# Attention interleaved with a SwiGLU block on one core: split gate and up operands made anew in the second half, stack loads by eight, attention steps spread over both halves, transposes one step later

## The chip, the cores and the metric

The kernel runs on one core of a Trainium2 chip. The metric is device time in microseconds (us) of one launch. Before the change three runs gave 1970.26, 1974.51 and 1974.52 us; the median is 1974.51 us. The core has a matrix engine (PE, with its weight loads listed as PEld), a vector engine (DVE), a scalar engine (ACT), a general engine (POOL) and a sync engine (SP), which in this kernel issues every DMA. Each engine works through its own instructions in order and waits where a semaphore says so.

## The reference, cut to what matters

```
x = A_x                                     # 2048 tokens, D = 576
g = sigmoid((x * gate_w).sum(-1))           # one gate per token
a = attention(x, wq, wk, wv, beta) @ wo     # 32 heads of 18, four segments of 512 tokens,
                                            # causal softmax inside a segment, plus a memory
                                            # read from the segments before it
b = (silu(x @ w_gate) * (x @ w_up)) @ w_down   # hidden width 4608
out = g * a + (1 - g) * b
```

All of it is float32. The kernel reaches that accuracy by splitting an operand into a rounded high part and a low part (the rest) and adding three products: high by high, high by low and low by high.

## The kernel before, in words

**Stages.** First comes a stage of about 230 us that makes queries, keys, values and the memory. It writes each query and key channel as three bfloat16 terms to a DRAM tensor `stk` (line 74; the stores are queued at lines 356 to 359) and the values to `vd`. Then come 72 tiles of the SwiGLU block with the attention woven in, and last a stage that multiplies by `wo` and mixes (lines 1085 to 1118).

**The SwiGLU tiles.** The loop at line 983 runs over two halves of 36 tiles. A half takes 1024 tokens as two blocks of 512, a tile takes 128 hidden channels, and both halves need the same weights. Gate and up weights of a tile, cut into two halves of 256 input channels, form a two by two block matrix. It is multiplied with the tokens by seven products instead of eight (`seven`, line 970): each product has six matmuls of 512 columns (line 975) and a seventh for the last 64 input channels (line 978). The seven left operands are sums and differences of weight blocks, each split into high and low. `w_make` (line 235) makes them: two raw weight loads of 256 KB each (`w_load`, line 198), four sums on POOL (line 243), seven high parts on ACT (line 247), seven low parts on DVE (line 250). It serves the first half only, where `keep` (line 253) also stores the seven operands of 256 KB each to DRAM (`wc`). In the second half `w_fetch` (line 690) loads them back, seven loads a tile (line 695). The operand pool `wop` has seven buffers, the raw pool four.

**The down product.** Every third tile (`q == 0`, called a group tile here) the hidden results of the three tiles before it are multiplied with `w_down` in 16 groups of nine matmuls (`down_group`, line 824). Three tiles, one of them a group tile, are called a triple here.

**The attention.** `att_gen` (line 782) is a generator. Two heads are a unit of five banks, and there are 64 units, so 320 banks. One step takes several banks each one stage further: `s_bank` multiplies queries and keys (PE, line 710) and takes the row maximum (DVE, line 716); `e_bank` takes the exponential (ACT, line 728) into a tile `pe` and masks it (POOL, line 736); `p_bank` makes a float16 high part (DVE, line 742) and low part (POOL, line 743) in a tile `p`, three steps after its scores (`PL`); `x_bank` transposes `p` by a DMA into `pt` (line 747), four steps after its scores (`XL`); `v_unit` multiplies with the values (PE, lines 758 and 759) and sums three terms (DVE, line 765), seven steps after the last scores of its unit (`VL`). The pool has 4 `pe`, 3 `p` and 8 `pt` buffers. For each unit the queries and keys are loaded from `stk` as a stack of 108 rows by ten DMAs (`stack_loads`, line 174; issued at line 790).

**What sets the order.** The order is written out by hand. A tile calls `tick` eight times, once after each product and once more, and `tick` calls `beat` (line 920). A beat first runs what was deferred to it (the parts of `w_make`, the loads, the splits), then its share of down groups (`SHARE`), and after every second of these an attention step if credit is there. Credit per slot comes from `TICK[half]`: the second number where down groups are pending, the first in other tiles. In the first half only beats 2 to 7 earn credit, and in a tile without groups beats 5 and 6 earn none (`QUIET`). With the numbers before, that gives 10 steps in a group tile and none in the others in the first half, 12 and four or five in the second half, and the attention ends in tile 31 of the second half. When the generator is empty, `c_open` (line 847) frees its pools and defers the loads for the last stage. SP gets its DMAs in that same order and starts none before the one ahead of it.

**The function tables of ACT.** Silu and exp need different tables. `exp_table` (line 967) runs a one element exp, so that the switch back from silu comes at a chosen place. Before the change it stands after the silu pair in every tile of the second half and in the group tiles of the first, and at the end of every third tile of the first half (line 1065).

## Time and profile before

| | |
|---|---|
| median of three runs | 1974.51 us (1970.26 to 1974.52) |
| profiled execution | 1969.58 us, of it span 1967.6 us |
| mean granted clock of PE | 0.973 |
| instructions | 35841 |
| matmuls | 11868 |
| DMA | 435.10 MB in 579305 packets |

The profile of one execution lists the instructions of each engine with start, duration and idle time ahead, and what ended that idle time. Times inside it count from the start of the span. The span is the time from the first to the last instruction; 1.98 us of the execution lie outside. Line 1032 (an ACT copy) runs once in each of the 72 tiles, at the end of the first product, so its starts mark the tiles. Line 742 (a DVE cast) runs once for each attention bank, so its count is the number of steps in a window. SP's instructions have no busy share; their rows show how long SP took to issue a DMA, not how long the transfer took.

### The profile page before, as it was taken

How to read it: one execution, taken by the hardware profiler on the slowest of the kernel's cores; microseconds unless marked ns; L12 is line 12 of the kernel's file. 1: busy time of each engine (PE TensorE's matmuls, PEld its weight loads, DVE VectorE, ACT ScalarE, POOL GpSimd, SP SyncE). 2: the span in 40 equal slices, each digit the busy share in tenths (PEclk: the TensorE clock that was granted, in tenths of full speed). 3: DMA queues.
4: the chain of work that ended last, by engine and by line, in shares of the span. 5: the costliest groups of instructions: out<-in, count | busy, mean ns of one | idle time of the engine just before them, and what ended most of it. 6: DMA issues, size and time to landing. Idle time of an engine off the chain costs nothing.

```text
span 1967.6 us, 35841 instructions
## 1 busy us (share of the span) xinstructions
PE 1777.4 (90%) x11868; PEld 1516.8 (77%) x11868; DVE 1222.8 (62%) x3001; ACT 999.6 (51%) x1927; POOL 824.3 (42%) x1058
## 2 busy tenths in 40 slices
PE   9999999898999999999888788788888878989999
PEld 7888887787878887788767676676766756768899
DVE  6655677675777676777755565555655655664445
ACT  7765565555555565555553544435544444454421
POOL 4443533453445444454444444444444444441021
PEclk9999999999999999999999999999998989989999
DMA  7644689889988898888998888979888798888634
GB/s 272 228 147 167 214 263 285 236 200 268 282 242 213 247 279 262 229 228 255 296 256 184 229 192 203 200 193 235 208 196 224 169 233 192 202 228 215 205 131 139
DMA packets 579305, 435.10 MB, mean 221 GB/s; under 512 B 418865, under 2 KB 461105, under 8 KB 579121
## 3 DMA queue, kind: packets, MB, share of 16 engines
q1 hardware_dynamic: 579120, 432.82, 80.8%
q8 instruction: 94, 1.54, 0.3%
q14 instruction: 91, 0.74, 0.1%
HBM read 210.32 MB, written 138.48 MB: 177 GB/s over the span
## 4 chain that ended last, share of the span: by engine, by line
PE 51%; DMA 22%; DVE 8%; issue 6%; ACT 5%; SPq 4%; POOL 4%; DVEq 0%; ACTq 0%; POOLq 0%
PE bank L975 21%; DMA pt<-p 15%; PE bank L834 13%; PE bank L137 8%; PE bank L978 3%; POOL p L743 2%; DMA draw<-in_wd_dram 2%; DVE p L742 2%; PE bank L710 2%; SPq L790 1%; SPq L747 1%; DVE ya L839 1%; PE bank L758 1%; DVE scr L716 1%; ACT L968 1%
## 5 line engine op out<-in xcount | busy, mean ns | idle before, releaser
L743 POOL TENSOR_TENSOR p<-pe,p 128x512 f16<-128x512 f32 x320 | 382.0, 1194 | 477.2 <-DVE p L742 476.9
L834 PE MATMUL bank<-dw,hh 128*128 128x320 f32 (+1 forms) x2304 | 496.0, 308 | 33.1 <-DVE ya L839 27.3
L834 PEld LDWEIGHTS bank<-dw,hh 128*128 128x128 f32 x2304 | 382.1, 191 | 58.2 <-DVE ya L839 40.1
L728 ACT ACTIVATE pe<-bank,mb 128x512 f32<-128x512 f32 (+3 forms) x512 | 244.9, 523 | 284.1 <-DVE mb L716 240.4
L834 PE MATMUL bank<-dw,hl 128*128 128x320 f32 (+1 forms) x1152 | 342.0, 297 | 0.3 <-DVE hl L115 0.3
L742 DVE CAST p<-pe 128x512 f16<-128x512 f32 x320 | 141.5, 442 | 303.8 <-DMA pt<-p 302.0
L716 DVE CUSTOM_DVE_ANT_0 scr<-bank,cm 128x512 bf16<-128x512 f32 (+3 forms) x512 | 246.2, 481 | 10.3 <-PE bank L710 3.4
L834 PEld LDWEIGHTS bank<-dw,hl 128*128 128x128 f32 x1152 | 219.5, 191 | 0.9 <-DVE hl L115 0.9
L978 PE MATMUL bank<-xr,rh 128*128 128x512 f32 x504 | 202.2, 401 | 9.2 <-DMA rh<-rc 9.1
L839 DVE TENSOR_TENSOR ya<-bank,ya 128x320 f32<-128x320 f32 x352 | 155.1, 451 | 82.9 <-PE bank L834 82.2
L736 POOL TENSOR_SCALAR_AFFINE_SELECT pe<-pe 128x256 f32<-128x256 f32 (+1 forms) x320 | 145.2, 454 | 105.0 <-ACT pe L728 103.0
L758 PE MATMUL bank<-v,pt 128*128 128x57 bf16 x1280 | 83.5, 190 | 55.5 <-DMA pt<-p 55.5
L1042 ACT ACTIVATE row<-bank 128x512 f32<-128x512 f32 x72 | 43.1, 599 | 172.4 <-PE bank L978 172.3
L710 PE MATMUL bank<-kst,qst 108*128 108x512 bf16 (+3 forms) x512 | 127.3, 310 | 3.7 <-DMA kst<-stk 2.8
L758 PEld LDWEIGHTS <-pt 128*128 128x128 f16 x1280 | 72.3, 97 | 70.1 <-DMA pt<-p 59.0
L243 POOL TENSOR_TENSOR ws<-raw 128x256 f32<-128x256 f32 x72 | 64.5, 896 | 145.1 <-DMA raw<-in_wf_dram 103.5
L978 PEld LDWEIGHTS bank<-xr,rh 128*128 128x128 f32 x504 | 97.9, 194 | 33.0 <-DMA rh<-rc 11.7
L918 DVE TENSOR_TENSOR hl<-row,hh 128x512 fp32r<-128x512 f32 x120 | 106.6, 888 | 20.9 <-ACT hh L917 20.5
L1032 ACT ACTIVATE bank<-bank 128x512 f32<-128x512 f32 x72 | 41.9, 581 | 131.3 <-PE bank L978 122.5
L1046 ACT ACTIVATE bank<-bank 128x512 f32<-128x512 f32 x72 | 41.9, 583 | 121.9 <-PE bank L978 121.6
L1047 DVE TENSOR_TENSOR row<-bank,row 128x512 f32<-128x512 f32 x72 | 49.6, 689 | 59.2 <-ACT bank L1046 59.2
L137 PE MATMUL bank<-xo,qhi 128*128 128x512 f32 x264 | 83.1, 396 | 0.0
(1689 smaller groups left out, 3869.7 us busy)
## 6 DMA issues: line engine op xcount, KB each, us to landing
rh<-rc SPq DMA_DIRECT2D x72, 336.0 KB
dc<-dw SPq DMA_DIRECT2D x36, 576.0 KB
dw<-dc SPq DMA_DIRECT2D x36, 576.0 KB
raw<-in_wf_dram SPq DMA_DIRECT2D x72, 256.0 KB
stk<-q SPq DMA_DIRECT2D x32, 384.0 KB
draw<-in_wd_dram SPq DMA_DIRECT2D x36, 288.0 KB
rc<-rt SPq DMA_DIRECT2D x42, 224.0 KB
vd<-vps SPq DMA_DIRECT2D x8, 912.0 KB
```

The lines of the kernel that those rows point to most:

```text
L137: nc.tensor.matmul(t, st[n], mv[n], start=(n == 0), stop=(n == 13))
L710: nc.tensor.matmul(t[:, c:c + w], qs[:KR, pr, P * i:P * i + P], ks[:KR, pr, 0:w], start=True, stop=True)
L716: nc.vector.tensor_tensor_reduce(scr[:, :w], t[:, c:c + w], cm[:, L - w:L], -SCALE, 3.0e38, OP.add, OP.min, m[:, k:k + 1])
L728: nc.scalar.activation(pe[:, c:c + w], t[:, c:c + w], AF.Exp, bias=m[:, k:k + 1], scale=SCALE)
L736: nc.gpsimd.affine_select(d, d, pattern=pat, compare_op=OP.is_ge, fill=0.0, base=0, channel_multiplier=1)
L742: nc.vector.tensor_copy(p[:, 0], pe)
L743: nc.gpsimd.tensor_sub(p[:, 1], pe, p[:, 0])
L758: nc.tensor.matmul(t[:, pr, i, :], pt[:, c], v, start=(n == 0), stop=False, skip_group_check=True)
L834: nc.tensor.matmul(t, p, q[:, cs], start=(n == 0), stop=(n == 3 * CH - 1))
L839: nc.vector.tensor_add(ya[:, i, cs], t, ya[:, i, cs])
L975: nc.tensor.matmul(t, w[:, p, z], x[z][:, q], start=first and n == 0, stop=False, skip_group_check=True)
L978: nc.tensor.matmul(t, rem[:, RPOS[j]], XR[j], start=False, stop=True, skip_group_check=True)
```

## The change

Six things change.

- In the second half only the first two tiles (`KEPT = 2`) load their operands from `wc`. For the other 34 tiles `w_make` runs again: raw loads, sums, high and low parts, without the stores. In the first half only the first two tiles store theirs.
- `TICK` changes, so that each tile of the first half that is no group tile gets two attention steps (a group tile 10 as before), and in the second half a group tile gets 10 and the others two or three.
- The stack of a unit is loaded by eight DMAs instead of ten, with the same rows. The first one of each kind takes 54 rows for both heads; for that the six pairs of terms are put in another order and the key terms are stored in reverse (`stk_store`).
- The transposes are issued five steps after the scores instead of four (`XL`), the product with the values follows eight steps after instead of seven (`VL`).
- There are 4 `p` buffers instead of 3, and 3 `pe` buffers instead of 4.
- `exp_table` stands after the silu pair in every tile of both halves.

With the new `TICK` and `VL` the attention has 333 steps instead of 332 and ends in tile 35 of the second half, the last one.

```diff
--- before.py
+++ after.py
@@ -37,10 +37,11 @@
 NB = 8 * NSEG
 NST = 2
 PL = 3
-XL = 4
-VL = 7
+XL = 5
+VL = 8
+KEPT = 2
 HALF = ((2, 3), (0, 1))
-TICK = ((0.0, 1.0), (0.76, 1.0))
+TICK = ((0.5, 1.0), (0.4, 0.85))
 QUIET = (5, 6)
 LEAD = 3
 SHARE = (0, 0, 2, 2, 3, 3, 3, 3)
@@ -73,7 +74,7 @@
     dram = pool(ctx, "dram", 1, space=bass.MemoryType.DRAM)
     stk = dram.tile([2, NSEG, D, 3, L], BF, name="stk")
     vd = dram.tile([NSEG, 2, P, 4, 16, 3, E], BF, name="vd")
-    wc = dram.tile([FT, 7, P, 4 * P], F32, name="wc")
+    wc = dram.tile([KEPT, 7, P, 4 * P], F32, name="wc")
     rc = dram.tile([FT // 4, 96, 4, 7 * P], F32, name="rc")
     xrd = dram.tile([7, P, L], F32, name="xrd")
     dc = dram.tile([FT, P, 2 * D], F32, name="dc")
@@ -173,20 +174,19 @@
 
     def stack_loads(u):
         s, b = divmod(u, 16)
-        q, k = (stk[kind, s, 2 * b * DH:2 * b * DH + 2 * DH].rearrange("(j r) z n -> r j z n", r=DH)
-                for kind in range(2))
-        tq, tk = qst[u % NST], kst[u % NST]
         r = []
-        for pr in range(2):
-            for z, n in ((0, 3), (1, 2)):
-                r0 = (0, 3 * DH)[z]
-                qz = q[:, pr, z]
-                r += [(tq[r0:r0 + n * DH, pr],
-                       bass.AP(tensor=qz.tensor, offset=qz.offset, ap=[qz.ap[0], [0, n]] + list(qz.ap)[1:])),
-                      (tk[r0:r0 + n * DH, pr], k[:, pr, 0:n])]
-            if pr == 0:
-                r += [(tq[5 * DH:KR], q[:, :, 2]), (tk[5 * DH:KR], k[:, :, 0])]
+        for kind, t, terms in ((0, qst, (0, 0, 1)), (1, kst, (2, 1, 2))):
+            d = stk[kind, s, 2 * b * DH:2 * b * DH + 2 * DH]
+            r.append((t[u % NST][0:3 * DH], d.rearrange("(j r) z n -> (r z) j n", r=DH)))
+            for n, z in enumerate(terms):
+                r.append((t[u % NST][(3 + n) * DH:(4 + n) * DH], d[:, z].rearrange("(j r) n -> r j n", r=DH)))
         return r
+
+    def stk_store(kind, s, a, b, q3):
+        d = stk[kind, s, a:b]
+        if kind:
+            d = bass.AP(tensor=d.tensor, offset=d.offset + 2 * L, ap=[d.ap[0], [-L, 3], [1, L]])
+        return d, q3
 
     def v_fetch(k):
         VP[k] = ap.tile([P, 4, 8, 3, E], BF, name="v")
@@ -232,9 +232,9 @@
     def r_fetch(f):
         nc.sync.dma_start(f32(rhs[f % 2][:96]).rearrange("p j n -> p (j n)"), rc[f // 4, :, f % 4])
 
-    def w_make(f):
+    def w_make(half, f):
         g, u = wraw_of.pop(f)
-        ops = wops[0, f] = [None] * 7
+        ops = wops[half, f] = [None] * 7
         a11, a12, a21, a22 = g[:, 0:2], g[:, 2:4], u[:, 0:2], u[:, 2:4]
         src = [a11, None, None, a12, None, None, a22]
 
@@ -257,8 +257,9 @@
                 (LEAD + 2, lambda: total(4, lambda: a11, lambda: a21)),
                 (LEAD + 4, lambda: total(5, lambda: a12, lambda: src[2]))]
         for j in range(7):
-            todo += [(LEAD + j, lambda j=j: high(j)), (LEAD + j + 2, lambda j=j: low(j)),
-                     (LEAD + j + 3, lambda j=j: keep(j))]
+            todo += [(LEAD + j, lambda j=j: high(j)), (LEAD + j + 2, lambda j=j: low(j))]
+            if half == 0 and f < KEPT:
+                todo.append((LEAD + j + 3, lambda j=j: keep(j)))
         return sorted(todo, key=lambda t: t[0])
 
 
@@ -353,10 +354,10 @@
             if ph is not None:
                 nc.vector.scalar_tensor_tensor(ph, t, 0.0, ph, op0=OP.max, op1=OP.add)
             if m < 4:
-                late.append((stk[u, s, m * P:m * P + P], q3))
+                late.append(stk_store(u, s, m * P, m * P + P, q3))
             else:
                 for kind in range(2):
-                    late.append((stk[kind, s, 512:D], q3[64 * kind:64 * kind + 64]))
+                    late.append(stk_store(kind, s, 512, D, q3[64 * kind:64 * kind + 64]))
 
         def v_step(s, hf, i):
             n = 288 + 2 * hf
@@ -636,7 +637,7 @@
                 wraw_of[0] = [w_load(0, u) for u in range(2)]
                 for z in range(2):
                     rhs.append(wop.tile([P, 7, P], F32R, name=f"rh{z}", bufs=1))
-                start = w_make(0)
+                start = w_make(0, 0)
             for n in range(8):
                 hf, i = divmod(n, 4)
                 flush()
@@ -721,7 +722,7 @@
             u, n = divmod(z, 5)
             m = mbs[u % 2]
             t = cur.pop(("t", z))
-            pe = ap.tile([P, L], F32, name="pe", bufs=4)
+            pe = ap.tile([P, L], F32, name="pe", bufs=3)
             for c, pr, i in SPLAN[n]:
                 w = P * (i + 1)
                 k = pr * 4 + i
@@ -738,7 +739,7 @@
 
         def p_bank(z):
             pe = cur.pop(("e", z))
-            p = cur["p", z] = ap.tile([P, 2, L], F16, name="p", bufs=3)
+            p = cur["p", z] = ap.tile([P, 2, L], F16, name="p", bufs=4)
             nc.vector.tensor_copy(p[:, 0], pe)
             nc.gpsimd.tensor_sub(p[:, 1], pe, p[:, 0])
 
@@ -786,7 +787,7 @@
                 if tau % 10 == 4 and sends:
                     nc.sync.dma_start(*sends.pop(0))
                 if n in (2, 3) and u + 1 < 2 * NB:
-                    for d in stack_loads(u + 1)[6 * (n - 2):4 * n - 2]:
+                    for d in stack_loads(u + 1)[4 * (n - 2):4 * n - 4]:
                         nc.sync.dma_start(*d)
                 z = tau - VL
                 if z % 20 == 0 and 0 <= z < N and z // 20 + 1 < 4 * NSEG:
@@ -989,15 +990,15 @@
                 groups += feed(half, f - 1)
             plan = []
             if nxt:
-                plan += w_make(nxt[1]) if nxt[0] == 0 else w_fetch(nxt[1])
+                plan += w_fetch(nxt[1]) if nxt[0] and nxt[1] < KEPT else w_make(*nxt)
                 if nxt != (0, 1):
                     plan.append((1 if nxt[1] else 10, lambda f=nxt[1]: r_fetch(f)))
                 for n, h in enumerate(BLOCKS.get(pos, ())):
                     plan += r_block(h, 4 * n)
-                if half == 0 and f + 2 < FT:
+                if f + 2 < FT:
                     wraw_of[f + 2] = [None, None]
                     for u in range(2):
-                        plan.append(((2, 5)[u], lambda u=u, f=f: wraw_of[f + 2].__setitem__(u, w_load(f + 2, u))))
+                        plan.append(((2, 5)[u] if f or not half else 5 + u, lambda u=u, f=f: wraw_of[f + 2].__setitem__(u, w_load(f + 2, u))))
             if pos == FT - 2:
                 X2, XR2 = [[None, None] for _ in range(7)], [None] * 7
                 plan += [(o + 8, fn) for o, fn in x_second(X2, XR2)]
@@ -1049,8 +1050,7 @@
             nc.scalar.activation(sg0, sg0, AF.Silu)
             seven(y, 5, False)
             nc.scalar.activation(sg1, y, AF.Silu)
-            if half or q == 0:
-                exp_table()
+            exp_table()
             tick()
             tick()
             seven(xx, 6, False)
@@ -1062,8 +1062,6 @@
                 split_by(2, hh[:, 0], hl[:, 0], sg0)
             split_by(3, hh[:, 1], hl[:, 1], sg1)
             tick()
-            if half == 0 and q == CH - 1:
-                exp_table()
             assert not groups
             if f == FT - 1:
                 groups += feed(half, f)
```

## The prediction

> **What bounds the kernel now.** I read the page first, then the starts of the 72 tiles, windows of whole triples, and SP's rows.
>
> ```profile
> span 1967.6 us, 35841 instructions
> PE 1777.4 (90%) x11868; PEld 1516.8 (77%) x11868; DVE 1222.8 (62%) x3001; ACT 999.6 (51%) x1927; POOL 824.3 (42%) x1058
> PE 51%; DMA 22%; DVE 8%; issue 6%; ACT 5%; SPq 4%; POOL 4%; DVEq 0%; ACTq 0%; POOLq 0%
> ```
>
> PE is busy for 90%, yet the chain that ended last lies on PE for only 51%, and on DMA for 22%. That is an average over unlike stages, so I cut the span at tile starts (line 1032).
>
> ```profile
> L1032 ACT ACTIVATE bank<-bank x31: 577/579/582, 266.8 to 898.6; 128x512 f32<-128x512 f32 x31
> ...
> L1032 ACT ACTIVATE bank<-bank x28: 582/582/598, 1035.1 to 1763.9; 128x512 f32<-128x512 f32 x28
> ...
> L742 DVE CAST p<-pe x96: 413/423/1314, 286.0 to 874.2; 128x512 f16<-128x512 f32 x96
> ...
> L742 DVE CAST p<-pe x191: 412/427/810, 1037.2 to 1762.8; 128x512 f16<-128x512 f32 x191
> ```
>
> 31 starts are 30 tiles, ten triples of the first half: 631.8 / 10 = 63.2 us each, with 9.6 attention steps. 28 starts are nine triples of the second half: 728.8 / 9 = 81.0 us each, with 21.2 steps. What would PE alone need? The end of the second half, where the attention is over, shows it, and one group tile with ten steps beside it (start and end, length, busy time and count of PE, PEld, DVE, ACT and POOL, granted clock, DMA share, GB/s):
>
> ```profile
> 1799.50:1810.60 11.10, 11.10 (x51) 9.19 (x49) 4.12 (x7) 7.29 (x12) 0.90 (x2) 1.00 0.95 298
> 1822.80:1853.50 30.70, 30.70 (x194) 28.34 (x193) 13.89 (x27) 9.35 (x15) 1.98 (x2) 1.00 0.48 139
> 898.60:933.30 34.70, 34.47 (x288) 31.18 (x287) 26.95 (x76) 16.70 (x36) 19.05 (x26) 1.00 0.80 202
> ```
>
> A bare tile is 11.1 us, a bare group tile 30.7, the group tile with ten steps 34.7: a step costs PE 0.40 us, and a triple with n steps has a floor of 52.9 + 0.40 n. The first half loses 63.2 - 56.7 = 6.5 us a triple, the second 81.0 - 61.4 = 19.6 us. The question is what takes the 19.6.
>
> ```profile
> DVE p L742 <- DMA pt<-p: 251.6, 111, 4.9
> ...
> SPq L747 <- POOL pe L736: 59.5, 71, 2.0
> SPq L747 <- POOL p L743: 19.0, 21, 1.8
> ```
>
> ```profile
> 1100.42 0.38 SPq L695 DMA_DIRECT2D wo__13533<-wc  x1
> 1100.85 0.80 SPq L790 DMA_DIRECT2D qst<-stk  x1
> 1101.71 0.48 SPq L790 DMA_DIRECT2D kst<-stk  x1
> 1102.24 0.78 SPq L790 DMA_DIRECT2D qst<-stk  x1
> 1103.06 0.75 SPq L790 DMA_DIRECT2D kst<-stk  x1
> 1103.85 0.48 SPq L790 DMA_DIRECT2D qst<-stk  x1
> 1104.38 0.31 SPq L790 DMA_DIRECT2D kst<-stk  x1
> 1104.79 1.27 SPq L747 DMA_TRANSPOSE pt<-p  x1
> ```
>
> ```profile
> L747 SPq DMA_TRANSPOSE pt<-p x192: 1231/1267/3547, 1033.6 to 1762.6; - x192
> ...
> L790 SPq DMA_DIRECT2D qst<-stk x190: 411/776/1823, 1044.6 to 1757.3; - x190
> L790 SPq DMA_DIRECT2D kst<-stk x190: 283/487/1345, 1045.4 to 1758.2; - x190
> ```
>
> In the nine triples (728.8 us) DVE stands for 251.6 us before the cast of line 742, because a transpose that must free a `p` buffer has not landed. The transposes are late because **SP is full**: its rows stand back to back, with 0.03 to 0.10 us between them. By medians it issues 192 x 1.267 = 243 us of transposes, 190 x 0.776 + 190 x 0.487 = 240 us of stack loads, and 189 operand loads (seven in each of 27 tiles) of 0.4 to 0.5 us, some 85 us. With some 80 other DMAs (half a microsecond each) and 0.08 us between all 840, that is about 675 of the 728.8 us, and at line 747 it waits for POOL in much of the rest (59.5 and 19.0 us). So the second half runs at the pace of SP, not of PE.
>
> **The change part by part.**
>
> *Operands made anew.* In 34 tiles of the second half seven loads become two, and 34 x 7 stores leave the first half. 476 transfers of 256 KB go and 68 come: 125 MB less and 18 MB more, of 435. What making them costs, the first half shows:
>
> ```profile
> 266.80:898.60 631.80, 85.02 (x210) 0.98 0.88 248
> ...
> 266.80:898.60 631.80, 104.85 (x212) 0.98 0.88 248
> ...
> 266.80:898.60 631.80, 105.15 (x120) 0.98 0.88 248
> ...
> 266.80:898.60 631.80, 74.62 (x156) 0.98 0.88 248
> ```
>
> These are the same window for line 247 (ACT, 0.405 us each), line 250 (DVE, 0.495), line 243 (POOL, 0.876) and line 728 (ACT exponentials, 74.62 / 96 = 0.78 us a step). A tile of the second half gains 7 x 0.405 = 2.8 us on ACT, 3.5 on DVE, 3.5 on POOL. In a group tile (ACT 16.7 us of 34.7 above) that lies beside PE. In the other tiles ACT is the engine to watch: the bare tile has 7.3 us, its tables included; plus 2.8, plus 2 to 2.5 steps at 0.78, that is 11.7 to 12.1; PE needs 11.1 + 2.5 x 0.40 = 12.1. A tile of the second half with three steps shows the same from the other end:
>
> ```profile
> 1022.60:1035.10 12.50, 12.50 (x63) 9.29 (x62) 8.52 (x23) 10.08 (x18) 4.95 (x7) 1.00 0.92 241
> ```
>
> PE fills its 12.5 us; with the operands made anew ACT has 10.1 + 2.8 = 12.9 and DVE 8.5 + 3.5 = 12.0; POOL has room (5.0 + 3.5). So PE, ACT and DVE stand abreast there.
>
> *Tables.* In the first half ACT now switches in all tiles: 12 more switches to silu and 12 back, inside the 7.3 us above.
>
> ```profile
> L1049 ACT ACT_TABLE_LOAD x60 | 77.0, 1283 | 1.1
> L968 ACT ACT_TABLE_LOAD x60 | 77.0, 1283 | 0.8
> ```
>
> That is 2.6 us in each of 12 tiles. The Trainium skill, "ScalarE: Activation LUTs", section "What ACT_TABLE_LOAD costs", gives 1283 ns for the load, as here, and 1380 ns for a drain on top. By that sentence each non-group tile would hold 2.8 us more ACT time. The rows show 0.8 and 1.1 us idle before all 60 loads of a kind together, so the sum here goes without the drain.
>
> *Even steps, SP's load.* A triple now has 14 or 15 steps. SP's part of a second half triple becomes 15 x 1.27 = 19.0 us of transposes, three stacks of eight loads, six raw loads and about eight others at half a microsecond, with 0.08 between some 53: about 42 us. The new loads (54 rows for both heads, 18 rows for both heads) have no row of their own; the stack rows bound them by 0.28 and 0.80 us, 6.7 to 19.2 us a triple. I take 0.5, nearest to the key row's 0.487; either way SP ends below 50 us. The first half has three `w_down` loads and stores and the blocks of line 226 more, and 21 stores less: under 50. SP no longer sets the pace.
>
> *Transposes a step later, buffers.* A transpose may wait a step longer for POOL, and the fourth `p` buffer gives DVE the same two steps until the buffer is needed: I count nothing beyond the 78.5 us of SP's waits, which lie in the 81.0. With three `pe` buffers instead of four the exponential waits for the subtraction of the step just before:
>
> ```profile
> ACT pe L728 <- POOL p L743: 33.1, 31, 2.8
> ...
> L743 POOL TENSOR_TENSOR p<-pe,p 128x512 f16<-128x512 f32 x320 | 382.0, 1194 | 477.2 <-DVE p L742 476.9
> ...
> L736 POOL TENSOR_SCALAR_AFFINE_SELECT pe<-pe 128x256 f32<-128x256 f32 (+1 forms) x320 | 145.2, 454 | 105.0 <-ACT pe L728 103.0
> ```
>
> The round is 0.78 (ACT) + 0.45 (mask) + 1.19 = 2.4 us, and in the dense part of a group tile steps come every 34.7 / 10 = 3.5 us or faster. It fits if DVE's cast is not late; bounds 0 and, if it is late as now, the third rival.
>
> *Stores of reversed keys.* The same bytes in three pieces a row, in a stage where SP and DMA have room; nothing, at most a few us.
>
> *The sum.* I take 36.5 us for a group tile (between 34.7 and 38.7) and 13.2 for the others (between 12.1 and 20.0): ACT's 12.9, and 0.3 for waits.
>
> ```profile
> 327.50:366.20 38.70, 36.26 (x287) 32.47 (x286) 26.01 (x76) 17.69 (x38) 20.63 (x32) 0.96 0.88 211
> 1241.80:1261.80 20.00, 15.39 (x98) 11.45 (x96) 10.27 (x28) 10.71 (x19) 8.22 (x12) 0.91 0.87 205
> ```
>
> The first is a group tile, the second a tile of the second half under SP's pace, which goes. I lean to the tile of 12.5 us above. A triple is then 36.5 + 2 x 13.2 = 63 us (floor 58.9). By stretches:
>
> ```profile
> L1032 ACT ACTIVATE bank<-bank x4: 582/582/582, 984.7 to 1035.1; 128x512 f32<-128x512 f32 x4
> ...
> L1032 ACT ACTIVATE bank<-bank x5: 582/582/582, 1799.5 to 1864.6; 128x512 f32<-128x512 f32 x5
> ```
>
> - up to 266.8: five steps and a few tables more, +4
> - first half, ten triples: 630 instead of 631.8, -2
> - 898.6 to 1035.1 (a triple, the break, three tiles without groups): 3 more in the first, 50 us to 40 in the last, -7
> - second half, nine triples: 567 instead of 728.8, -162
> - 1763.9 to 1864.6 (five tiles, before with seven steps in all): 113 instead of 101, +12
> - the end: two steps more; and the loads for `wo` start in the last tile instead of tile 31, so part of them is bare: +2 and +4
>
> That is -149: a span of 1819, 1821 us with the 2 us outside. The profiled execution (1969.6) lies 4.9 us under the median of the runs; I add most of that back and **forecast 1825 us**.
>
> **The rivals.** *ACT lags in the non-group tiles.* Two engines abreast with waits between them lose more than half a microsecond. At 15.5 us 47 tiles add 2.3 us each: 1825 + 108 = 1933. For it: ACT's order is fixed, and the two silus with two table loads of 1.28 us stand as one block in it. By the drain that the page of the Trainium skill states the tile would be 13.2 + 2.8 = 16.0, and the time 1957 (0.02 of this case's chance). Against: the 12.5 us row.
>
> *A step costs the same wherever it stands* (the slower side). From 63.2 us at 9.6 steps to 81.0 at 21.2 the slope is 1.53 us a step. If that belongs to the loop of cast, subtraction, transpose and buffer, not to SP, then moving steps moves their price: ten triples +67, the triple after +6, the three tiles -8, nine triples -85, the last two triples +35, start and end +12: +27, and the 4 to the median: 2001 us. It decides from 69.8 us a triple on (63 + 149 / 22). For it: DVE's 251.6 us at that very buffer. Against: SP's rows without a gap.
>
> *Three `pe` buffers bind.* POOL waits 476.9 us for the cast, 1.5 us a step. If that passes to ACT in the ten steps of 22 group tiles, and a third of it to PE, the group tiles take 5 us longer each: 1825 + 110 = 1935. Against: with SP free the cast waits less.
>
> *The operands come late all the same.*
>
> ```profile
> POOL ws L243 <- DMA raw<-in_wf_dram: 90.3, 13, 10.9
> ```
>
> In the first half POOL waits 90.3 us in 30 tiles for raw loads, 3.0 a tile. If 33 tiles of the second half pay that on PE: 1825 + 99 = 1924. Against: with 107 MB less to move the loads land sooner.
>
> **How the numbers follow.** Forecast (1780 to 1880) 0.66; ACT lags 0.11; `pe` binds 0.06; operands late 0.05; steps cost the same 0.12. Within 0.3%, about what a measurement of this kernel can tell from no change, end 0.02 of the lagging ACT and 0.01 of the steps. Faster 0.86, same 0.03, slower 0.11. The range starts at 1780 (a triple at 61, two above the floor) and ends at 1935, where the lagging ACT, `pe` and the late operands stand.
>
> **What would show it.** SP's rows in the second half have gaps; DVE's wait for `pt` falls from 251.6 us to under 60; triples of both halves take 61 to 66 us; line 250 runs some 480 times; PE's clock in the second half rises from 0.95. I am wrong if non-group tiles take over 15 us with ACT full, if ACT waits at line 728 for line 743 above 100 us, or if group tiles pass 40 us.

## The result and the profile after

The changed kernel takes 1822.75 us, median of four runs (1821.75 to 1823.75); the kernel before takes 1974.51 us beside it (four runs, 1970.26 to 1978.05). The ratio is 0.9232, 95% interval 0.9213 to 0.9251: 152 us less. The forecast was 1825.

The page of the profile after: span, busy time by engine, the granted clock in 40 slices, the bytes, the chain that ended last.

```profile
span 1820.0 us, 34926 instructions
...
PE 1731.5 (95%) x11868; PEld 1488.8 (82%) x11868; DVE 1412.3 (78%) x3239; ACT 1101.1 (60%) x2201; POOL 975.1 (54%) x1194
...
PEclk9999999999999999999998999999999999999999
...
DMA packets 524002, 328.05 MB, mean 180 GB/s; under 512 B 411184, under 2 KB 460336, under 8 KB 523824
...
PE 56%; ACT 15%; DVE 14%; issue 6%; POOL 4%; DMA 4%; SPq 1%; DVEq 0%; ACTq 0%; POOLq 0%
```

DMA has gone from 22% of the chain to 4%. DVE, ACT and POOL do more work than before (1412.3 against 1222.8 us on DVE), and yet the span is 147.6 us shorter: their added work lay beside PE's. Line 1032 of before is line 1033 here, so the same cuts at tile starts give the triples, and the two windows give busy time and count of PE, PEld, DVE, ACT and POOL, granted clock, DMA share and GB/s.

```profile
L1033 ACT ACTIVATE bank<-bank x31: 582/582/601, 269.8 to 909.4; 128x512 f32<-128x512 f32 x31
...
L1033 ACT ACTIVATE bank<-bank x28: 572/582/592, 1043.1 to 1602.6; 128x512 f32<-128x512 f32 x28
...
L743 DVE CAST p<-pe x136: 414/422/869, 1043.1 to 1602.6; 128x512 f16<-128x512 f32 x136
```

```profile
269.80:909.40 639.60, 601.87 (x4214) 510.53 (x4214) 527.60 (x1223) 406.64 (x809) 375.08 (x483) 1.00 0.82 186
1043.10:1602.60 559.50, 544.30 (x3916) 461.30 (x3916) 472.88 (x1106) 351.32 (x703) 336.79 (x406) 1.00 0.75 165
```

639.6 / 10 = 64.0 us a triple in the first half, 559.5 / 9 = 62.2 in the second, and there PE is busy for 544.3 of 559.5 us at a granted clock of 1.00: but for 15 us, PE sets the pace again. The stretches of the forecast's sum, in us of the profiled execution:

| stretch | before | forecast | after |
|---|---|---|---|
| up to tile 3 | 266.8 | 270.8 | 269.8 |
| first half, ten triples | 631.8 | 630 | 639.6 |
| tiles 33 to 39 | 136.5 | 129.5 | 133.7 |
| second half, nine triples | 728.8 | 567 | 559.5 |
| tile 66 to the start of the last tile | 100.7 | 112.7 | 106.2 |
| the rest | 103.0 | 109 | 111.2 |
| span | 1967.6 | 1819 | 1820.0 |

SP in the second half: its transposes and stack loads, and then 10 us of its timeline (start, duration, what).

```profile
L748 SPq DMA_TRANSPOSE pt<-p x135: 1231/1239/2487, 1045.1 to 1598.9; - x135
...
L791 SPq DMA_DIRECT2D qst<-stk x108: 293/321/1847, 1046.4 to 1585.8; - x108
L791 SPq DMA_DIRECT2D kst<-stk x108: 265/331/623, 1050.0 to 1591.3; - x108
```

```profile
1203.15 1.23 SPq L748 DMA_TRANSPOSE pt<-p  x1
1204.48 0.86 SPq L822 DMA_DIRECT2D dw<-dc  x1
1205.44 0.38 SPq L200 DMA_DIRECT2D raw<-in_wf_dram  x1
1205.92 1.23 SPq L748 DMA_TRANSPOSE pt<-p  x1
1211.70 0.34 SPq L200 DMA_DIRECT2D raw<-in_wf_dram  x1
1212.13 1.42 SPq L791 DMA_DIRECT2D qst<-stk  x4
```

Before, the rows stood back to back; here SP ends a transpose at 1207.15 and starts the next DMA at 1211.70. The waits of the whole run that matter (us in total, times, longest):

```profile
POOL pe L737 <- ACT pe L729: 355.3, 219, 4.8
ACT pe L729 <- POOL p L744: 327.6, 184, 4.4
POOL p L744 <- DVE p L743: 172.1, 145, 2.9
...
PEld bank L835 <- DVE ya L840: 40.7, 46, 6.9
...
PE bank L835 <- DVE ya L840: 27.6, 36, 6.7
...
DVE p L743 <- DMA pt<-p: 5.3, 5, 1.8
```

DVE's wait for a transpose, 302.0 us in the whole run before and 251.6 of it in nine triples, is 5.3. A new one has come: ACT waits 327.6 us for the subtraction that frees a `pe` buffer. The two rows of line 835 are waits of PE, and of its weight loads, for DVE's sums of the down product (line 840); several runs below turn on them.

### The profile page after: what moved, and what is told of

It reads as the page before. It is cut to its first block, busy times and chain, and to the rows that moved or that the text cites. A ratio compares the mean times of both kernels' runs of the same rounds, so it can differ in the third digit from the quotient of the medians.

```text
span 1820.0 us, 34926 instructions
## 1 busy us (share of the span) xinstructions
PE 1731.5 (95%) x11868; PEld 1488.8 (82%) x11868; DVE 1412.3 (78%) x3239; ACT 1101.1 (60%) x2201; POOL 975.1 (54%) x1194
## 3 DMA queue, kind: packets, MB, share of 16 engines
q1 hardware_dynamic: 523824, 325.83, 73.4%
## 4 chain that ended last, share of the span: by engine, by line
PE 56%; ACT 15%; DVE 14%; issue 6%; POOL 4%; DMA 4%; SPq 1%; DVEq 0%; ACTq 0%; POOLq 0%
PE bank L976 21%; PE bank L835 15%; PE bank L138 10%; PE bank L979 3%; ACT L969 3%; ACT L1050 3%; PE bank L711 2%; PE bank L759 2%; POOL p L744 2%; ACT pe L729 2%; DVE scr L717 1%; DVE hl L919 1%; DVE p L743 1%; ACT row L1052 1%; ACT row L1050 1%
## 5 line engine op out<-in xcount | busy, mean ns | idle before, releaser
L835 PE MATMUL bank<-dw,hh 128*128 128x320 f32 (+1 forms) x2304 | 500.3, 310 | 35.7 <-DVE ya L840 27.6
L744 POOL TENSOR_TENSOR p<-pe,p 128x512 f16<-128x512 f32 x320 | 396.0, 1237 | 172.1 <-DVE p L743 172.1
L729 ACT ACTIVATE pe<-bank,mb 128x512 f32<-128x512 f32 (+3 forms) x512 | 247.7, 522 | 327.7 <-POOL p L744 327.6
L835 PEld LDWEIGHTS bank<-dw,hh 128*128 128x128 f32 x2304 | 384.5, 191 | 59.7 <-DVE ya L840 40.7
L737 POOL TENSOR_SCALAR_AFFINE_SELECT pe<-pe 128x256 f32<-128x256 f32 (+1 forms) x320 | 152.0, 475 | 360.9 <-ACT pe L729 355.3
L979 PE MATMUL bank<-xr,rh 128*128 128x512 f32 x504 | 196.6, 390 | 0.0
L743 DVE CAST p<-pe 128x512 f16<-128x512 f32 x320 | 151.1, 472 | 5.3 <-DMA pt<-p 5.3
L919 DVE TENSOR_TENSOR hl<-row,hh 128x512 fp32r<-128x512 f32 x120 | 117.9, 983 | 22.9 <-ACT hh L918 22.4
L243 POOL TENSOR_TENSOR ws<-raw 128x256 f32<-128x256 f32 x140 | 131.3, 938 | 5.7 <-DVE mb L717 3.4
L979 PEld LDWEIGHTS bank<-xr,rh 128*128 128x128 f32 x504 | 94.6, 188 | 20.2
L1047 ACT ACTIVATE bank<-bank 128x512 f32<-128x512 f32 x72 | 41.9, 582 | 84.5 <-PE bank L979 84.4
L353 POOL TENSOR_TENSOR q<-qr,q 128x512 bf16<-128x512 f32 x36 | 44.8, 1243 | 70.1 <-ACT q L352 58.5
```

The source lines that it names most:

```text
L729: nc.scalar.activation(pe[:, c:c + w], t[:, c:c + w], AF.Exp, bias=m[:, k:k + 1], scale=SCALE)
L737: nc.gpsimd.affine_select(d, d, pattern=pat, compare_op=OP.is_ge, fill=0.0, base=0, channel_multiplier=1)
L743: nc.vector.tensor_copy(p[:, 0], pe)
L744: nc.gpsimd.tensor_sub(p[:, 1], pe, p[:, 0])
L835: nc.tensor.matmul(t, p, q[:, cs], start=(n == 0), stop=(n == 3 * CH - 1))
L979: nc.tensor.matmul(t, rem[:, RPOS[j]], XR[j], start=False, stop=True, skip_group_check=True)
```

## The experiments

**What was to be told apart.** My theory: the second half ran at the pace at which SP issues DMAs. So fewer or shorter issues must gain, and fewer bytes alone must not. The rivals: the bytes (DMA share 0.87 before), the price of a step that is the same wherever it stands, the `pe` buffers, and ACT in the tiles without groups. First each part was put alone into the kernel before, then each part was taken out of the changed kernel alone. All ratios are to runs of the kernel before on the same chip beside them. "SP" in the table is the part of a stretch in which SP issues: its issue times added up over the rows of the trace, and 0.08 us between rows, over the length.

| kernel | median us | ratio, 95% interval | triple, half 1 | triple, half 2 | SP, half 1 | SP, half 2 |
|---|---|---|---|---|---|---|
| before | 1974.51 | | 63.2 | 81.0 | 0.91 | 1.00 |
| changed | 1822.75 | 0.9232 (0.9213 to 0.9251) | 64.0 | 62.2 | 0.72 | 0.64 |
| before, stack loads by eight | 1858.71 | 0.9407 (0.9363 to 0.9452) | 59.1 | 73.4 | 0.85 | 0.90 |
| before, even steps | 1938.29 | 0.9804 (0.9764 to 0.9843) | 72.7 | 63.8 | 0.97 | 0.95 |
| before, operands made anew | 1883.55 | 0.9517 (0.9477 to 0.9557) | 60.3 | 73.9 | 0.70 | 0.98 |
| before, half the bytes of operands | 1957.80 | 0.9903 (0.9870 to 0.9936) | 63.3 | 79.5 | 0.92 | 1.00 |
| changed, all operands kept | 1835.60 | 0.9312 (0.9260 to 0.9363) | 67.1 | 60.0 | 0.91 | 0.82 |
| changed, uneven steps | 1827.22 | 0.9266 (0.9224 to 0.9308) | 57.6 | 71.0 | 0.60 | 0.78 |
| changed, stack loads by ten | 1859.62 | 0.9420 (0.9394 to 0.9446) | 67.8 | 62.2 | 0.83 | 0.82 |
| changed, old depth and buffers | 1799.57 | 0.9124 (0.9082 to 0.9166) | 63.5 | 60.6 | 0.73 | 0.67 |
| changed, old buffers alone | 1822.87 | 0.9250 (0.9205 to 0.9296) | 65.5 | 61.2 | 0.70 | 0.64 |
| changed, old depth alone | 1808.83 | 0.9164 (0.9143 to 0.9184) | 64.3 | 60.7 | 0.72 | 0.66 |
| changed, value product at 7 alone | 1810.41 | 0.9182 (0.9147 to 0.9217) | 64.4 | 60.6 | 0.71 | 0.65 |
| old depth and buffers, steps placed anew | 1790.39 | 0.9073 (0.9052 to 0.9094) | 60.1 | 64.2 | 0.67 | 0.74 |

### Before, with the stack loads by eight alone

The change's `stack_loads`, `stk_store` and line 790 in the kernel before; the bytes stay as they are.

```diff
-                    for d in stack_loads(u + 1)[6 * (n - 2):4 * n - 2]:
+                    for d in stack_loads(u + 1)[4 * (n - 2):4 * n - 4]:
```

> The kernel before with one edit: the stack of a unit is loaded by eight DMAs instead of ten (and the key terms stored in reverse for it). Bytes, steps and all else stay. Theory (SP's issue time sets the pace of the second half): in the changed kernel a stack load takes SP 0.37 us in the mean (232 loads, 86.9 us), before 0.65; a unit costs SP 8 x 0.45 = 3.6 us instead of 10 x 0.73 = 7.3, gaps included, and a triple of the second half has 4.2 units. SP gains 15 us a triple; the triples fall from 81.0 us to between 66 and 72, where the next engine takes over, and the total by 80 to 130 us, to 1840 to 1890. Rival (the bytes of the DMAs set the pace): the bytes are the same, the triples stay at 80 to 82 us, the total within 10 us of before. Rival (a step costs the same wherever it stands): as the second, no change.

1858.71 us, 116 us less from this part alone. The stack loads in the second half (shortest, median and longest issue in ns), and the tile starts:

```profile
L789 SPq DMA_DIRECT2D qst<-stk x152: 265/331/1991, 998.2 to 1635.2; - x152
L789 SPq DMA_DIRECT2D kst<-stk x152: 265/326/847, 1002.4 to 1641.0; - x152
```

```profile
L1031 ACT ACTIVATE bank<-bank x28: 580/582/597, 991.3 to 1651.6; 128x512 f32<-128x512 f32 x28
```

Before, it was 190 at 0.776 and 190 at 0.487 us; now 152 at 0.331 and 152 at 0.326: 240 us become 100, of issue time alone. 660.3 us for nine triples instead of 728.8: 73.4 each, a little above the 66 to 72 that I gave, with SP still issuing for 0.90 of the time. The first half gains too, 59.1 us a triple instead of 63.2. The bytes can't be the cause, since they are the same, and the DMA engines were no less busy (share 1.01 in the nine triples, counted by when a transfer starts, and 0.87 before); that rival falls here.

### Before, with half the bytes of the stored operands

```diff
-                nc.sync.dma_start(f32(ops[j]).rearrange("p a k n -> p (a k n)"), wc[f, j])
+                nc.sync.dma_start(f32(ops[j])[:, 0].rearrange("p k n -> p (k n)"), wc[f, j][:, :2 * P])
...
-                    nc.tensor.matmul(t, w[:, p, z], x[z][:, q], start=first and n == 0, stop=False,
+                    nc.tensor.matmul(t, w[:, 0 if half else p, z], x[z][:, q], start=first and n == 0, stop=False,
```

> The kernel before, with the same number of operand loads in the second half but half the bytes in each: only the high parts are loaded back, and the products of the second half read the high part in place of the low one, so the low parts of gate and up weights are left out there. Theory (SP's issue time): 128 rows are issued either way, SP's time stays, the triples of the second half stay within 2 us of 81.0, total within 20 us of before. Rival (bytes): a triple moves 2.75 MB less of 16.7; at the same rate the triples fall to 68, the total by 120 us or more.

1957.80 us, in a kernel that leaves out the low parts of the gate and up weights in the second half. By its page of the profile it moved 33 MB less, with the same number of issues:

```profile
DMA packets 579304, 402.07 MB, mean 206 GB/s; under 512 B 418864, under 2 KB 493360, under 8 KB 579120
```

```profile
L1032 ACT ACTIVATE bank<-bank x28: 582/582/599, 1035.1 to 1750.6; 128x512 f32<-128x512 f32 x28
```

715.6 us for nine triples, 79.5 each: SP still issues without a gap, and 33 MB are worth 17 us.

### Before, with the operands made anew alone

```diff
-                plan += w_make(nxt[1]) if nxt[0] == 0 else w_fetch(nxt[1])
+                plan += w_fetch(nxt[1]) if nxt[0] and nxt[1] < KEPT else w_make(*nxt)
```

The other edits of that part (`KEPT = 2`, the raw loads in both halves, stores for two tiles only) are those of the change.

> The kernel before with one edit: the operands of all but two tiles are made anew in the second half, not stored and loaded back. Steps uneven as before, ten stack loads. Theory (SP): a triple of the second half keeps 21.2 steps; 21 loads of 0.61 us become 6 of 0.5, so SP falls by 10 us from 81 to 71; with PE's floor of 61.4 the triples take 71 to 74 us, and the first half, rid of 21 stores a triple, falls from 63.2 to 60 to 62. Total 1860 to 1900. Rival (bytes): 5.5 MB of 16.7 a triple go and 1.6 come; at the same rate the triples would fall from 81 to 62, total about 1790. Rival (ACT and DVE): the non-group tiles with 4 to 5 steps and the operands hold 7.3 + 2.8 + 4.5 x 0.78 = 13.6 us on ACT and no more than 14 on DVE, well under their share of 71.

1883.55 us, 91 less. Second-half triples at 73.9 us with SP still issuing for 0.98 of the time: the ten stack loads and 21 transposes remain. The 107 MB that are gone don't bring the 1790 us of the bytes' rival.

### Before, with the even steps alone

```diff
-TICK = ((0.0, 1.0), (0.76, 1.0))
+TICK = ((0.5, 1.0), (0.4, 0.85))
```

The place of `exp_table` is the change's too.

> The kernel before with the attention steps spread evenly (and the switch back to the exp table in every tile, as that needs); operands still stored and loaded back, ten stack loads. Theory (SP): a triple of the second half with 15 instead of 21.2 steps has 15 x 1.49 of transposes + 30 x 0.73 of stack loads + 21 x 0.61 of operand loads + 9 x 0.6 = 62.5 us on SP, close to what PE, ACT and DVE need (63), so it falls to 64 to 68 us; the first half, with 14 steps, 21 stores and 6 raw loads, has 14 x 1.49 + 28 x 0.73 + 27 x 0.65 + 8 = 67 us on SP and rises from 63.2 to 67 to 71. Total 1870 to 1930. Rival (a step costs 1.53 us wherever it stands): the halves trade one for one, first half triples 70, second half 71, total 1970 to 2000.

1938.29 us, 36 less, a little over the range that I gave. The starts of the tiles in the first half:

```profile
L1032 ACT ACTIVATE bank<-bank x31: 581/582/597, 271.1 to 998.3; 128x512 f32<-128x512 f32 x31
```

72.7 us a triple instead of 63.2: now the first half, with its 21 stores a triple, is where SP is full (0.97), and 95 of the 155 us that the second half gains are lost again. From before to this kernel a step costs 9.5 / 4.4 = 2.2 us in the first half and 17.2 / 6.2 = 2.8 in the second, more than the 1.53 between the halves of one kernel.

### The changed kernel with all operands kept

```diff
-KEPT = 2
+KEPT = 36
...
-                if f + 2 < FT:
+                if half == 0 and f + 2 < FT:
```

> The changed kernel with one edit undone: the operands of all 36 tiles are stored in the first half and loaded back in the second (KEPT = 36), so all 435 MB are moved again; even steps, eight stack loads and the pipeline stay. Theory (SP): a triple of the second half has 15 x 1.39 + 24 x 0.45 + 21 x 0.61 + 6 x 0.6 = 48 us on SP, well under 62, so SP still doesn't set the pace there: 61 to 64 us (62.2 in the changed kernel). The first half has 14 x 1.5 + 22 x 0.5 + 27 x 0.65 + 12 x 0.6 = 57 of 64 us on SP: 64 to 67. Total 1815 to 1860: the operands made anew are worth little once the stack loads are eight and the steps even. Rival (bytes): the 107 MB come back, triples of the second half rise by 6 us or more, total above 1880.

1835.60 us, 13 more than the changed kernel. Its two halves (columns as in the windows above):

```profile
271.50:942.10 670.60, 612.10 (x4214) 517.55 (x4214) 524.10 (x1223) 407.64 (x808) 371.43 (x482) 0.98 0.98 258
1074.50:1614.90 540.40, 537.27 (x3917) 463.59 (x3917) 361.87 (x915) 294.18 (x514) 227.21 (x298) 1.00 0.99 239
```

The second half is the fastest of all these kernels, 60.0 us a triple (I had given 61 to 64), with the DMA share at 0.99 and PE busy for 537 of 540 us. So a DMA share near 1 held PE up for 3 us at most there, and making operands anew costs that half 2 us a triple; what it gains is in the first half, where the stores go (67.1 against 64.0). Alone in the kernel before it was worth 91 us, here 13: most of SP's relief can be had only once.

### The changed kernel with the steps as before

```diff
-TICK = ((0.5, 1.0), (0.4, 0.85))
+TICK = ((0.0, 1.0), (0.76, 1.0))
```

The place of `exp_table` is that of before too.

> The changed kernel with the old step spread (none outside the group tiles in the first half, 21 a triple in the second) and the old places of the switch to the exp table; operands made anew and eight stack loads stay. Theory (SP was the bound and is so no more): SP has about 52 us a triple in the second half, so the triples there follow their floor of 61.4 and DVE's load in the tiles with 4 to 5 steps (4.1 + 5.0 + 4.5 x 1.4 = 15.4 us): 66 to 71 us; the first half 58 to 60 us; total 1800 to 1850. Rival (even steps are themselves the gain): second half triples stay near 80, total above 1880.

1827.22 us, 4.5 more than the changed kernel, with intervals that overlap: **spreading the steps evenly is worth nothing measurable here.** The triples move by much, and against each other: 57.6 us instead of 64.0 at 9.6 steps (a little under the 58 to 60 that I gave), 71.0 instead of 62.2 at 21.1. The price of a step is 6.4 / 4.4 = 1.45 us in the first half and 8.8 / 6.1 = 1.44 in the second. What makes it up, the first half shows (with 96 steps here, and with 140 above in the changed kernel):

```profile
266.90:842.50 575.60, 570.66 (x3790) 500.79 (x3789) 445.93 (x1033) 348.53 (x711) 294.82 (x386) 1.00 0.72 177
```

PE is busy 31 us longer for 44 steps, 0.71 us a step and not 0.40; the other 33 us are idle time of PE (5 here, 38 in the changed kernel). In the changed kernel's first half PE waits for ACT's copy of line 1033:

```profile
PE bank L976 <- ACT bank L1033: 19.6, 18, 1.3
```

The second half here has the matmuls and, but for one, the steps of the kernel before, and PE was busy for 583.2 us of it at a granted clock of 0.99, against 613.9 us at 0.95 before. So some 3 us of the gain of a triple went with the clock; what set the clock no run here shows.

### The changed kernel with the stack loads by ten

```diff
-        for kind, t, terms in ((0, qst, (0, 0, 1)), (1, kst, (2, 1, 2))):
+        for pr in range(2):
+            for z, n in ((0, 3), (1, 2)):
```

The rest of `stack_loads`, the order of the stored terms and the loop that issues them are those of before too.

> The changed kernel with one edit undone: ten stack loads a unit again (keys stored in their old order). Theory (SP has room now): a triple of the second half has 15 x 1.39 + 30 x 0.73 + 6 x 0.47 + 6 x 0.6 = 49 us on SP, one of the first 14 x 1.5 + 28 x 0.73 + 6 x 0.7 + 9.5 = 55, both under the 62 to 64 they last; the triples rise by 0 to 3 us and the total ends between 1823 and 1880. The stack loads, worth 116 us alone, are worth under 60 once the rest is there. Rival (they are the gain): total above 1890.

1859.62 us, 37 more, inside the range. All of it is in the first half, 67.8 us a triple, 3.8 more where I had given at most 3; the second stays at 62.2. SP's stack loads there, and what DVE waits for:

```profile
L798 SPq DMA_DIRECT2D qst<-stk x140: 422/777/2274, 286.0 to 941.6; - x140
L798 SPq DMA_DIRECT2D kst<-stk x140: 302/496/1390, 286.8 to 942.5; - x140
```

```profile
DVE p L750 <- DMA pt<-p: 35.0, 22, 4.7
...
PE bank L842 <- DVE ya L847: 25.3, 17, 3.3
```

SP issues for 0.83 of that half, far from full, and yet transposes come late (35.0 us against 5.3), and PE waits longer for DVE's sums (25.3 against 5.4 us). The second half has the same share, 0.82, and loses nothing. Cut by tile, the trace shows a difference: in the first half the group tiles take 39.9 us instead of 36.6, the other tiles 14.2 and 13.7 instead of 13.6 and 13.7, and SP issues for 0.93 of the group tiles. In the second half they stay at 36.1 us, with SP at 0.86. So where the time goes SP is nearly full, which the mean over a triple hides; that this is the cause was not tried by a run of its own.

### The changed kernel with the old depth and buffers

```diff
-XL = 5
-VL = 8
+XL = 4
+VL = 7
...
-            pe = ap.tile([P, L], F32, name="pe", bufs=3)
+            pe = ap.tile([P, L], F32, name="pe", bufs=4)
...
-            p = cur["p", z] = ap.tile([P, 2, L], F16, name="p", bufs=4)
+            p = cur["p", z] = ap.tile([P, 2, L], F16, name="p", bufs=3)
```

> The changed kernel with the pipeline edits undone: transposes four steps and the product with the values seven steps after the scores, 3 p and 4 pe buffers. Theory (they count for nothing beyond SP's waits): within 12 us of the changed kernel; ACT's wait for POOL at the pe buffers (327.6 us) falls under 100, and PE does not gain by it. Rival (a transpose a step later is what keeps SP and DVE apart): DVE's wait for pt comes back above 100 us, triples rise by 2 us or more, total above 1860.

1799.57 us: 23 us faster than the changed kernel. My theory, that these four edits count for nothing within 12 us, falls.

```profile
ACT pe L729 <- DVE mb L717: 195.4, 91, 3.9
...
PEld bank L835 <- DVE ya L840: 20.3, 25, 5.9
...
PE bank L835 <- DVE ya L840: 14.0, 22, 5.7
...
ACT pe L729 <- POOL p L744: 4.2, 4, 2.0
```

ACT's wait for a `pe` buffer is gone, 4.2 instead of 327.6 us. But PE's wait for the sums of the down product is halved too, and that isn't a matter of `pe`. Three more runs take the four edits apart.

### The old buffers alone

Four `pe` and three `p` buffers as in the diff above, the depths as in the change.

> The changed kernel with 3 p and 4 pe buffers, transposes still a step later. The p buffer that the cast needs is then handed to the transpose only one step before. Theory: DVE waits for pt again, 100 us or more in all, and as DVE is now busy 83% of a triple the triples rise by 1 to 4 us; total 1840 to 1900. Rival (pe is the scarcer of the two, as ACT's 327.6 us of waiting says): ACT's wait goes and the total falls below 1815.

1822.87 us: neither range holds it.

```profile
PEld bank L835 <- DVE ya L840: 44.5, 44, 7.3
...
DVE p L743 <- DMA pt<-p: 34.0, 28, 3.0
...
PE bank L835 <- DVE ya L840: 31.9, 35, 7.1
...
ACT pe L729 <- POOL p L744: 23.4, 18, 3.5
```

ACT's wait falls from 327.6 to 23.4 us and the time doesn't move. With three `p` buffers and the later transpose DVE waits a little for `pt` again (34.0); PE's wait for DVE's sums is as long as in the changed kernel (31.9 against 27.6).

### The old depth alone

`XL = 4`, `VL = 7`, with the change's buffers.

> The changed kernel with transposes four and the product with the values seven steps after the scores, but with its 4 p and 3 pe buffers. With all four pipeline edits undone the kernel took 1799.57 us, with the buffers alone undone 1822.87. Theory (a ring that is reused one step later costs the 23 us: pe with three buffers in the changed kernel, p with three and the later transpose in the other): pe still has three, ACT waits for POOL 250 us or more, total 1812 to 1826. Rival (the later transpose itself costs them): total 1795 to 1805.

1808.83 us, 14 less than the changed kernel and between my two ranges. So of the 23 us some 14 come from the depths. The other 9 come with the buffers, and only beside the old depths: beside the later ones they changed nothing (1822.87). The intervals of this kernel's ratio and of that with depths and buffers put back (0.9143 to 0.9184, 0.9082 to 0.9166) overlap, so the 9 is not certain. ACT's wait for `pe` is 310.4 us here: 306 us more idle time of an engine, worth some 9.

### The value product at seven alone

```diff
-VL = 8
+VL = 7
```

> The changed kernel with one number undone: the product with the values follows seven steps after the scores, not eight; the transposes stay five steps after, with 4 p and 3 pe buffers. With both numbers undone the kernel took 1808.83 us, with neither 1822.75. Theory (the later product costs the 14 us: its sum on DVE then falls in steps where down groups wait for DVE; PE waits for DVE at line 835 for 28.6 us between 1046 and 1592 us in the changed kernel, for 6.3 with both undone): second half triples fall from 62.2 to 60.7 as with both undone, total 1804 to 1814. Rival (the later transpose costs them): total 1818 to 1826.

1810.41 us, as with both depths put back: the later transpose shows no cost, and the later product with the values costs some 12 us (the intervals of the ratios, 0.9147 to 0.9217 and 0.9213 to 0.9251, just touch). They lie in the second half, 60.6 us a triple instead of 62.2. In the whole run PE's waits for the sums are those of the faster kernels:

```profile
PEld bank L835 <- DVE ya L840: 25.5, 27, 5.9
...
PE bank L835 <- DVE ya L840: 18.2, 22, 5.6
```

In the changed kernel they are 40.7 and 27.6 us. Of the five kernels that differ in depths and buffers alone, the two with `VL = 8` have them long (27.6 and 31.9 us on PE), the three with 7 short (18.2, 16.1 and 14.0). Why a product one step later puts DVE's sums (line 840) where PE waits for them was not tried.

### The old depth and buffers, with the steps placed anew

In the first half 12 steps in group tiles and none beside, in the second 12 and three; the attention ends before the last two tiles.

```diff
-TICK = ((0.5, 1.0), (0.4, 0.85))
+TICK = ((0.0, 1.0), (0.5, 1.0))
...
-                credit[0] += 0.5 if k is None else TICK[half][busy] * (half or k > 1)
+                credit[0] += 0.5 if k is None else TICK[half][busy]
```

Depths, buffers and the place of `exp_table` are those of before.

> The changed kernel with its pipeline edits undone, and the steps put where they were cheapest: in the first half 12 in each group tile (beats 0 and 1 earn credit too) and none elsewhere, with the old places of the exp table; in the second half 12 and 3, so that the attention ends in tile 33. Theory (a step in a tile without groups costs more than one in a group tile, as ACT and DVE are full there: first half triples took 57.6 us with ten steps in the group tile alone and 64.0 with 14 of which four stood outside): first half triples 59 to 61, second half 61 to 64, the last stage 8 us shorter as the wo loads start earlier; total 1755 to 1785. Rival (a step costs 1.4 us in any tile): the halves trade, only the end gains, 1788 to 1800.

1790.39 us, the lowest median of all, 32 us under the changed kernel. My range is missed by 5 us, and the rival's, 1788 to 1800, holds it. Against the kernel with the old depth and buffers it is 9 us less, and the intervals of the two ratios overlap (0.9052 to 0.9094, 0.9082 to 0.9166).

```profile
L1033 ACT ACTIVATE bank<-bank x31: 580/583/586, 267.7 to 868.5; 128x512 f32<-128x512 f32 x31
```

```profile
L1033 ACT ACTIVATE bank<-bank x28: 578/586/595, 999.8 to 1577.2; 128x512 f32<-128x512 f32 x28
```

First-half triples are at 60.1 us, as expected, and PE no longer waits for line 1033 there; second-half triples, with 18.0 steps instead of 15.1, rise from 60.6 to 64.2, 1.2 us a step, where I had counted less. So the halves trade, 34 us less against 32 more, as the rival says: that a step is cheaper in a group tile doesn't show in the total. The stretch from the start of the last tile is 102.2 us instead of 110.5, since its loads start two tiles earlier, but the tile ahead of it takes 20.2 us instead of 12.1, of which PE waits 6.5 for the load of an operand (`rh`): the end gains 1 us. Another 4 us lie ahead of tile 3.

## Why the prediction was right, and where it was not

**SP set the pace: right, and shown.** Less issue time with the same bytes gained 116 us; fewer bytes with the same issues gained 17; with SP at 0.64 to 0.72 DVE's wait for `pt` went. SP was fuller than the sum of medians said (675 of 728.8 us): the rows of those triples add up to 659 us of issues and 70 us between them, with 9 us in gaps over 0.15 us. The Trainium skill, "DMA: Bandwidth & Descriptors", section "Issuing engines are not separate DMA queues", says of the time on the sequencer to initiate a DMA that it "is usually small relative to the DMA itself". How long one of these DMAs took by itself no run here shows; but 844 issues in 729 us, small or not, were together the bound.

**1825 forecast, 1822.75 measured: in part luck.** The stretches of the sum were off by between -7.5 and +9.6 us and cancel to 1 us, and the pipeline edits, put at nothing, cost 23 us that terms put too high elsewhere made up: without these edits the kernel took 1799.57.

**Second half, 567 us: measured 559.5.** Group tiles took 36.1 us (I took 36.5), the others 12.6 and 13.4 (13.2).

**First half, 630 us: measured 639.6.** The sum took the same tile times there; group tiles took 36.6 us, the others 13.6 and 13.7, not 13.2. The sum didn't say that SP cost this half anything, and the run with eight stack loads shows that it did (59.1 us a triple instead of 63.2). The changed kernel with the old steps is at 57.6, and the 4.4 steps a triple moved into this half, at 1.45 us, took the gain and a little more.

**The floor of 52.9 + 0.40 n: too low in n.** It came from the difference of two single group tiles. The runs give 0.71 us of PE and 1.45 in all for a step with SP relieved. So the rival that a step costs the same wherever it stands was close in the slope (1.53), and wrong about the time: it held the level fixed, and SP's relief lowered the level. The even steps, which I counted in the 162 us, gain nothing once the stack loads and the operands are changed.

**The parts don't add up.** Alone they are worth 116, 91 and 36 us, 243 together; the change, with the pipeline edits that cost 23, gives 152. Three ways to relieve one queue share what it holds.

**Pipeline edits at nothing: wrong, 23 us.** This is the step that failed, hidden in the total by others that came out better. The later product with the values, some 12 us, I hadn't priced at all. The third rival, three `pe` buffers, is not there at 110 us: ACT's wait came, but the old buffers (`pe` and `p` together) gave 0 us beside the later depths and some 9, not certain, beside the old ones.

**New stack loads at 0.5 us: 0.33 us.** These are medians; with the longer ones the mean is 0.375 in the second half. It lies in the lower half of the bounds.

**Operands made anew.** ACT's part is as computed (0.39 us a high part, taken 0.405). DVE's low parts took 135.37 / 189 = 0.72 us, not 0.495 (below); in the second half they lie beside PE, and the run with all operands kept sets the price at 2 us a triple.

**The break and the end.** Tiles 33 to 39 were 4 us over the forecast, the five tiles after tile 66 were 6 under, the end 2 over.

**The signs and the other rivals.** SP's gaps, DVE's 5.3 us, triples of 64.0 and 62.2, the clock at 1.00: all came. ACT didn't lag in the tiles without groups: they took 13.7 us in the mean and 14.7 at most, not 15.5. The operands weren't late: POOL's wait for raw loads, 90.3 us before, is gone. One sign was badly chosen: that I am wrong if ACT waits at line 728 for line 743 above 100 us. It waited 327.6, and the time was right; with the old buffers 304 us of that wait went and the time stayed.

## What to carry to other kernels

Add up the issue time of a DMA queue stage by stage and look at the gaps between its rows: here the queue without gaps was the bound, though the profile showed the wait on another engine and the DMA share was high. Cut by tile too: a mean of 0.83 hid tiles at 0.93. Price moved work with what a step costs once the bound is gone, and try each of several reliefs of one queue alone and each taken out, since together they gain less than their sum. Idle time on an engine with slack is no price: 304 us of ACT's waits went here and the time stayed, while 9 us of PE's (27.6 against 18.2) went with 12.

## What the runs showed of the hardware

**The time to issue a DMA depends on its form.** In the same kernel but for the stack loads SP took 0.777 and 0.496 us (medians) for each of ten loads a unit, and 0.342 and 0.346 for each of eight, with the same bytes: over the whole of each trace ten loads take 6.5 us and eight 3.1. The first pair is the first half of the changed kernel with the loads by ten, the second the first half of the changed kernel.

**DVE's subtraction of two operands in SBUF takes longer when it begins while POOL computes.** Line 250 (128x256) in the two halves of the changed kernel (DVE's time and count on that line, granted clock, DMA share, GB/s):

```profile
269.80:909.40 639.60, 130.24 (x210) 1.00 0.82 186
1043.10:1602.60 559.50, 135.37 (x189) 1.00 0.75 165
```

That is 0.62 and 0.72 us each, against 0.495 before, for the same operation. The timeline of DVE and of POOL in the changed kernel:

```profile
1204.00 0.42 DVE L250 TENSOR_TENSOR wo__15842<-ws,wo__15842 128x256 fp32r<-128x256 f32 x1
...
1214.04 0.96 DVE L250 TENSOR_TENSOR wo__16021<-ws,wo__16021 128x256 fp32r<-128x256 f32 x1
```

```profile
1204.13 0.55 POOL L737 TENSOR_SCALAR_AFFINE_SELECT pe<-pe 128x256 f32<-128x256 f32 x1 [1.01 <-ACT pe L729]
1204.66 1.16 POOL L744 TENSOR_TENSOR p<-pe,p 128x512 f16<-128x512 f32 x1
...
1213.79 0.92 POOL L243 TENSOR_TENSOR ws<-raw 128x256 f32<-128x256 f32 x1
```

The first began before POOL's mask and ended beside it, and took 0.42 us; the second began beside a POOL sum and took 0.96. All rows of this line, in the traces of both kernels, say the same: the 391 that began while POOL stood idle took 0.41 to 0.43 us, also where POOL began beside them, and the 351 that began while POOL worked took 0.83 us in the mean. The Trainium skill, "GPSIMD Engine Reference", section "1. Specifications", says that POOL shares its interfaces to SBUF with VectorE, with contention where a DVE instruction has two SBUF inputs; these rows agree, and give the size. It was seen in the traces, not tried by a run of its own.
